# Token loads as two transfers of 48 rows, the sum of f written ahead of its rounded copy, and 24 nudged operations in a spectral transform with a gated FFN on one core

## The chip, the core and the metric

The kernel runs on one core of a Trainium2 chip. The metric is the device time of one execution in microseconds; lower is better. TensorE (PE) does the matrix products, VectorE (DVE), ScalarE (ACT) and GpSimd (POOL) do the element-wise work, and SyncE (SP) issues nearly all DMA transfers.

## The reference

Eight sequences of 3008 tokens with 256 channels go through a spectral layer, and its output through a gated feed-forward layer.

```python
X = np.fft.rfft(x, axis=1)                     # x: (8, 3008, 256), float32
Yr = Xr @ w_r - Xi @ w_i + b_r
Yi = Xr @ w_i + Xi @ w_r + b_i
Yr = sign(Yr) * maximum(abs(Yr) - 0.01, 0)     # and the same for Yi
y = np.fft.irfft(Yr + 1j * Yi, n=3008, axis=1)
g = y @ w_gate                                 # 24064 tokens, 256 -> 1536
silu = g / (1 + exp(-g))
out = (silu * (y @ w_val)) @ w_out             # 1536 -> 256
```

## The kernel before

The program has two stages: the transform (0 to 520 us of the span) and the gated FFN (519 to 2555 us, matmul line L791), which the change leaves as it is.

**Tokens.** The 3008 tokens of a sequence are cut into factors for a Fourier transform done by matrix products. The input is laid out by the host so that one array `xp[b, k]` holds the tokens of sequence b for a pair of chunks k (eight pairs a sequence) as 128 rows of 1024 floats. Rows 0 to 47 and 64 to 111 carry tokens (47 and a zero row each); the other rows are zero. One transfer of 128 rows (512 KB) brings a pair: L332 for sequence 0 (`x_first`), L463 for the others (`x`, written as "scratch<-xp" in the rows). `stage_a` (L470, operation names `first k` for sequence 0 and `tiles k` for the others) multiplies the two 48-row halves by the constant `wa` into two banks; 16 block transposes a sequence on DVE (`turn`, L475) put the result into `d`. The constant `wa` comes with its own small transfer at L309.

**Slots.** There are 8 sequences of 12 pairs of frequencies, 96 slots j in all. Each runs through this chain:

- `second` (PE, L513) writes a bank `ps_b` of 128x512 from `d`;
- `f` (ACT, L576) copies one half of that bank; `f_sum` (DVE, L577) adds the other half to it, the rows "f<-f,ps_b";
- `f_hi` (ACT, L575) rounds the whole bank to the short format; `f_lo` (DVE, L578) forms what the rounding left out, bank less `f_hi`;
- `flat_hi` (ACT, L579) and `flat_lo` (POOL, L580) do the same for the sum f, and `sum` (PE, L520) multiplies them;
- `spread` (DVE, L524) and `mix` (PE, L535) add to the products, `gather` (ACT, L547), `clip` (DVE, L585) and `shrink` (POOL, L586) do the thresholding, `y_hi` and `y_lo` (L587, L594) split again, `back` (PE, L557 and L559) transforms back, `z` and `store` (L598, L599) put the result into `d` in DRAM.

`second j+1` overwrites `ps_b` after `f_lo j` and `f_sum j` have read it.

In the same time PE does `stage_a` for the next sequence, and the last transform step of the one before (`z_in`, transfers at L639 from `d` in two pieces of 48 rows, rows 0 to 47 and 64 to 111, 192 KB each, and the products at L650). DVE and POOL also convert FFN weights (`bits`, L418 to L424).

**Order.** Each operation has a key: its slot times 5.5, moved by a number of its kind from the table `SHIFT`. A planner walks through the operations by key, chooses an engine where there are two, and so fixes each engine's order; nothing is reordered at run time. An operation that is written later and touches the same PSUM bank or buffer waits for the one ahead of it, on whatever engine it runs.

**Start.** All eight `x_first` pairs are loaded first, with `wr`, `wf`, `bias`, `wj` and `raw_i` behind them, and then the pairs of sequence 1 (`x 0` and on). PE does some products on a cleared tile (L719, L721) ahead of `first 0`, and fills its waits with products on such tiles (L740 and L742, "idle").

Of the kernel before, what the change touches and what calls it, by code (L numbers as in the profile page):

```python
# [17 lines left out]
P = 128  # L18
# [27 lines left out]
SHIFT = {"add": -0.5, "lower": 0.5, "third": -0.5, "turn5": 0.12, "turn4": 0.06, "turn0": -0.44, "y_hi": -0.37, "f": -0.5, "out": 0.75, "spread": 0.0, "back": -0.19, "raw": 0.37, "second": 0.06, "y_lo": 0.68, "shrink": 0.44, "z_in": 0.06, "mix": 0.5, "wr": -1.0, "turn1": 0.0, "tiles": 0.56, "turn6": -0.31, "wo": 0.06, "x_sum": -0.5, "sum": -0.5, "flat_lo": -0.12, "xt1": 0.18, "x": 0.12, "store": 0.37, "turn": -0.32, "wm": -0.12, "bits down": -0.5, "upper": 0.25, "wj": -0.12, "kept": -1.0, "negate": 0.25, "turn3": 0.12, "unit": 0.56, "wm_hi": -0.12, "z": 0.5, "bias": -0.44, "wi_lo": -0.06, "turn2": -0.18, "x_hi": -0.5, "clip": -0.5, "xt0": -0.25, "wa": 0.06, "warm": 0.25, "bits up": -1.5}  # L46
# [4 lines left out]
WARM = 1  # L51
# [198 lines left out]
def spectral_ffn(ctx: ExitStack, tc: tile.TileContext, xp, w_r, w_i, cb, wup_raw, wdn_raw, ca, cf, ci, cq, out):  # L250
# [15 lines left out]
    with ExitStack() as tail:  # L266
        last = tail.enter_context(tc.tile_pool(name="last", bufs=2, side="right"))
        with ExitStack() as one:
            finish, stored = transform(one, tc, front, ring, last, ps_, feed, xp, w_r, w_i, cb, wup_raw, wdn_raw, ca, cf, ci, cq, w21, wup_d, wdn_d, xt_d, d2)
# [6 lines left out]
def transform(ctx, tc, front, ring, last, ps_, feed, xp, w_r, w_i, cb, wup_raw, wdn_raw, ca, cf, ci, cq, w21, wup_d, wdn_d, xt_d, d2):  # L276
# [16 lines left out]
    places = [scratch[:, i * T : (i + 2) * T] for i in (3, 5)]  # L293
# [21 lines left out]
    def head(plan):  # L315
# [816 lines left out]
```

## Time and profile before

| | us |
|---|---|
| median of 3 runs (2557.44 to 2557.63) | 2557.52 |
| the profiled execution | 2556.73 |
| its span | 2554.9 |
| PE busy in it | 2544.8 |
| DVE / POOL / ACT busy | 2064.7 / 2082.1 / 1705.0 |

The page of the profile gives busy times and shares for the span. Its 40 slices of 63.9 us show PE at 9 tenths or more in every slice and a granted clock of 9 tenths or more in every slice; the DMA digits are 6 to 8 in the first eight slices and 4 to 5 behind them. The views by window cut the same sums to stretches of our choice. A row of the timeline is one instruction, or some of the same form in a row (x4), with its start, its length, and in brackets how long its engine stood idle ahead of it and what ended that.

### The profile page before, as it was taken

What the parts mean: (1) busy time and instruction counts of PE and PEld (TensorE: products, weight loads), DVE (VectorE), ACT (ScalarE), POOL (GpSimd) and SP (SyncE); (2) the same over time, 40 slices, a digit from 0 to 9 for tenths busy, and PEclk for the clock granted to TensorE, in tenths of its full rate; (3) what the DMA queues carried; (4) which work ended last, traced back from release to release, by engine and by line L of the source; (5) the groups of instructions that cost most, each with busy time, mean ns of one, the idle gap of its engine ahead of it and who ended that gap; (6) DMA issues with size and microseconds to landing.
All of it is one profiled execution on the core that took longest, in us unless ns stands there. A gap on an engine that the chain in (4) does not pass through costs nothing.

```text
span 2554.9 us, 45902 instructions
## 1 busy us (share of the span) xinstructions
PE 2544.8 (100%) x16534; PEld 2136.0 (84%) x16534; DVE 2064.7 (81%) x2998; ACT 1705.0 (67%) x3342; POOL 2082.1 (81%) x1595
## 2 busy tenths in 40 slices
PE   9999999999999999999999999999999999999999
PEld 6888888978888888888888888888888888888899
DVE  7989898677877877887788788878887888788887
ACT  6888888966666665666656666666666566656665
POOL 5777777568888888888888888888888888888886
PEclk9999999999999999999999999999999999999999
DMA  6788888855445444544444444444444444444453
GB/s 236 246 293 277 287 281 273 252 206 183 159 154 177 163 154 153 175 157 151 160 158 150 141 163 163 151 142 163 163 151 143 162 163 146 142 158 158 151 182 123
DMA packets 133924, 460.57 MB, mean 180 GB/s; under 512 B 13632, under 2 KB 58944, under 8 KB 133696
## 3 DMA queue, kind: packets, MB, share of 16 engines
q1 hardware_dynamic: 133552, 457.53, 54.0%
q8 instruction: 131, 2.15, 0.4%
q14 instruction: 97, 0.79, 0.1%
q10 hardware_dynamic: 144, 0.10, 0.0%
HBM read 366.61 MB, written 90.96 MB: 179 GB/s over the span
## 4 chain that ended last, share of the span: by engine, by line
PE 97%; DVE 1%; DMA 1%; ACT 0%; issue 0%; POOL 0%; SPq 0%; DVEq 0%
PE bank L791 79%; PE mixb L535 5%; PE ps_b L513 3%; PE ps_s L520 3%; PE ps_z L559 3%; PE ps_x L650 2%; PE ps_a L470 2%; PE bank L1037 0%; DMA x_first<-xp 0%; DMA scratch<-xp 0%; PE ps_z L557 0%; DVE y_lo L594 0%; ACT t L547 0%; DVE f_lo L578 0%; POOL t L586 0%
## 5 line engine op out<-in xcount | busy, mean ns | idle before, releaser
L791 PE MATMUL bank<-x_near,wup 128*128 128x512 f32 (+1 forms) x4032 | 1035.8, 386 | 0.4 <-DVE bank L964 0.2
L811 POOL TENSOR_TENSOR h_parts<-more,h_parts 128x512 fp32r<-128x512 f32 (+1 forms) x572 | 847.2, 1495 | 101.8 <-ACT h_parts L807 100.7
L791 PEld LDWEIGHTS bank<-x_near,wup 128*128 128x128 f32 x4032 | 751.0, 188 | 152.7 <-DVE bank L964 3.9
L791 PE MATMUL bank<-h_parts,wdn 128*128 128x512 f32 (+1 forms) x3024 | 835.3, 385 | 0.0
L811 POOL TENSOR_TENSOR h_parts<-hidden,h_parts 128x512 fp32r<-128x512 f32 (+1 forms) x431 | 563.7, 1319 | 213.7 <-ACT h_parts L807 176.9
L791 PEld LDWEIGHTS bank<-h_parts,wdn 128*128 128x128 f32 x3024 | 564.9, 188 | 108.5 <-POOL h_parts L811 0.3
L807 ACT CAST h_parts<-hidden 128x512 fp32r<-128x512 f32 (+1 forms) x433 | 265.5, 613 | 451.0 <-DVE hidden L937 449.7
L791 PE MATMUL bank<-x_parts,wup 128*128 128x512 f32 (+1 forms) x2016 | 525.7, 384 | 0.0
L937 DVE TENSOR_TENSOR hidden<-hidden,bank 128x512 f32<-128x512 f32 (+1 forms) x576 | 375.8, 674 | 78.1 <-PE bank L791 69.6
L791 PEld LDWEIGHTS bank<-x_parts,wup 128*128 128x128 f32 x2016 | 375.4, 188 | 71.7 <-DVE bank L964 1.7
L832 DVE TENSOR_TENSOR sums<-sums,bank 128x512 f32<-128x512 f32 (+1 forms) x357 | 240.2, 673 | 234.3 <-PE bank L791 234.3
L807 ACT CAST h_parts<-more 128x512 fp32r<-128x512 f32 (+1 forms) x572 | 349.3, 611 | 39.3 <-DVE more L802 28.4
L935 ACT ACTIVATE hidden<-bank 128x512 f32<-128x512 f32 (+1 forms) x432 | 252.6, 585 | 114.6 <-PE bank L791 113.9
L802 DVE TENSOR_TENSOR more<-hidden 128x512 f32<-128x512 f32 (+1 forms) x286 | 291.9, 1059 | 0.0
L802 DVE TENSOR_TENSOR more<-hidden,more 128x512 f32<-128x512 f32 (+1 forms) x286 | 257.7, 901 | 0.0
L942 ACT COPY bank<-bank 128x512 f32<-128x512 f32 (+1 forms) x288 | 161.6, 561 | 109.3 <-DVE hidden L937 103.9
L964 DVE TENSOR_TENSOR bank<-hidden,bank 128x512 f32<-128x512 f32 (+1 forms) x288 | 196.9, 684 | 36.3 <-PE bank L791 23.5
L586 POOL TENSOR_TENSOR t<-t,y 128x512 f32<-128x512 f32 x94 | 129.3, 1376 | 70.1 <-DVE y L585 63.1
L950 ACT COPY hidden<-bank 128x512 f32<-128x512 f32 (+1 forms) x288 | 167.6, 582 | 2.2
L547 ACT COPY t<-mixb 64x256 f32<-64x256 f32 x384 | 140.9, 367 | 22.0 <-PE mixb L535 17.1
L243 POOL TENSOR_TENSOR x_near<-xf,x_near 128x512 fp32r<-128x512 f32 (+1 forms) x112 | 142.3, 1286 | 5.2 <-PE bank L791 4.8
L986 DVE TENSOR_TENSOR hidden<-hidden,bank 128x512 f32<-128x512 f32 (+1 forms) x144 | 97.4, 676 | 42.7 <-PE bank L791 42.4
(111 smaller groups left out, 3104.1 us busy)
## 6 DMA issues: line engine op xcount, KB each, us to landing
wup<-wup_d SPq DMA_DIRECT2D x288, 896.0 KB, 4.7
scratch<-xp SPq DMA_DIRECT2D x59, 512.0 KB, 4.9
out<-o SPq DMA_DIRECT2D x88, 256.0 KB, 6.1
d<-z SPq DMA_DIRECT2D x84, 256.0 KB, 3.9
z_in<-d SPq DMA_DIRECT2D x112, 192.0 KB, 5.1
xt_d<-xt SPq DMA_DIRECT2D x56, 376.0 KB, 4.7
xf<-xt_d SPq DMA_DIRECT2D x15, 1024.0 KB, 7.8
wup_d<-wup SPq DMA_DIRECT2D x12, 896.0 KB, 5.8
```

The source lines that it names most:

```text
L243: low = lambda: eng.tensor_tensor(part[:, 1, :h], src, f32(part[:, 0, :h]), op=ALU.subtract)
L547: nc.scalar.copy(t()[64 * half : 64 * half + 64, k * C : (k + 1) * C], mixb[64 * k : 64 * k + 64, half * C : (half + 1) * C])
L791: nc.tensor.matmul(o, lhsT=weights[w], rhs=parts[x], start=start and i == 0, stop=stop and i == 2, skip_group_check=True)
L802: v.tensor_tensor(at(o, h), at(a, h), at(b, h), op=ALU.subtract)
L807: act.copy(pair[i][:, 0, :h], at(i, h))
L811: eng.tensor_tensor(pair[i][:, 1, :h], at(i, h), f32(pair[i][:, 0, :h]), op=ALU.subtract)
L832: v.tensor_tensor(o, o, spare[:, :h], op=ALU.add)
L935: act.activation(at(i, h), src, AF.Silu)
L937: v.tensor_tensor(at(i, h), at(i, h), src, op=ALU.mult)
L942: act.copy(b3[:, :h], b1[:, :h])
L950: act.copy(m5, b2[:, :h])
L964: v.tensor_tensor(b2[:, :h], m5, b3[:, :h], op=ALU.add)
```

## The change

The change has four parts.

1. **Transfers of 48 rows.** Every pair of tokens is loaded as two transfers, rows 0 to 47 and rows 64 to 111, 192 KB each, in place of one of 128 rows. The zero rows are not moved any longer. `wa` travels with the first pair (48 rows of 1088 floats), and POOL copies it from there to its own tile; its transfer is gone.
2. **f_sum ahead of f_hi.** After planning, the order in which the operations are written is gone through: where it can be done without passing another operation of ACT, or of DVE, `f_hi j` is put behind `f_sum j`.
3. **Tables.** `SHIFT`, `BIAS` and the keys of `wr` and `wj` have new values, and 24 single operations get a further shift of 0.25 or 0.5 slot (`NUDGE`).
4. **Start.** The clearing of the tile for PE's first products goes from POOL to DVE, with other numbers of these products; the differences and sums of the weights (`wm`, `wm_lo`) may go to DVE or POOL; the second of two banks is cleared by an operation of its own.

```diff
-BIAS = {'y_lo POOL': 0.2, 'z DVE': 1.7, 'flat_lo DVE': 1.2, 'shrink DVE': 1.5}
+BIAS = {"y_lo POOL": 0.1, "z DVE": 0.7, "flat_lo DVE": 1.5, "shrink DVE": 1.6}
+NUDGE = {"shrink 33": -0.5, "flat_lo 17": -0.25, "tiles 41": 0.25, "turn 0 3": 0.5,
...
-        key += SHIFT.get(name.split()[0], 0) * SLOT
+        key += (SHIFT.get(name.split()[0], 0) + NUDGE.get(name, 0)) * SLOT
...
+    HALVES = slice(0, 48), slice(64, 112)
...
-            nc.sync.dma_start(box[k], xp[0, k, :, : 2 * T])
+            wide = 2 * T if k else 2 * T + 64
+            if not k:
+                box[k] = scratch[:, 5 * T : 5 * T + wide]
+            for rows in HALVES:
+                nc.sync.dma_start(box[k][rows], xp[0, k, rows, :wide])
...
-        plan.add("wa", "SP", 0.45, -39.5, [], load_wa, 2.0)
+        plan.add("wa", "POOL", 0.2, -39.5, ["x_first 0"], lambda: [g.tensor_copy(wa[rows], box[0][rows, 2 * T :]) for rows in HALVES])
...
-        plan.add("wm 1", "POOL", 1.23, 0.5 * SLOT, ["wj"], combine(1, ALU.subtract))
+        plan.add("wm 1", either, None, 0.5 * SLOT, ["wj"], combine(1, ALU.subtract), wide=True)
...
     def fetch(t, b, k):
-        nc.sync.dma_start(t, xp[b, k, :, : 2 * T])
+        for rows in HALVES:
+            nc.sync.dma_start(t[rows], xp[b, k, rows, : 2 * T])
...
     order = plan.order()
+    for j in range(B * NP):
+        names = [name for name, _ in order]
+        i, k = names.index(f"f_hi {j}"), names.index(f"f_sum {j}")
+        between = {engine for _, engine in order[i + 1 : k]}
+        if i < k and "ACT" not in between:
+            order.insert(k, order.pop(i))
+        elif names.index(f"f {j}") < i < k and "DVE" not in between:
+            order.insert(i, order.pop(k))
```

**The start on PE.** This is PE's order from the later pairs of sequence 0 to `second 1`; L470 (L477 after) is `first` and `tiles`, L513 (L520) is `second`, L740 and L742 (L760 and L762) are the filling products. Before:

```order
L470 MATMUL ps_a<-x_first,wa 64x512 x20
L470 MATMUL ps_a<-scratch,wa 64x512 x4
L740 MATMUL mixb_130<-warm,wa 64x128 x2
L740 MATMUL mixb_131<-warm,wa 64x128 x2
L740 MATMUL mixb_130<-warm,wa 64x128 x2
L740 MATMUL mixb_131<-warm,wa 64x128 x2
L513 MATMUL ps_b<-wf,d_0_115 128x128 x2
L742 MATMUL mixb_130<-warm 128x128 x2
L513 MATMUL ps_b<-wf,d_0_115 128x128 x2
L742 MATMUL ps_x_249<-warm 128x128 x5
L470 MATMUL ps_a<-scratch,wa 64x512 x4
L513 MATMUL ps_b<-wf,d_0_115 128x128 x4
```

and after:

```order
L477 MATMUL ps_a<-x_first,wa 64x512 x12
L728 MATMUL mixb_131<-warm 128x512
L520 MATMUL ps_b<-wf,d_0_115 128x128 x2
L762 MATMUL mixb_130<-warm 128x128
L477 MATMUL ps_a<-scratch,wa 64x512 x4
L760 MATMUL mixb_130<-warm,wa 64x128 x4
L477 MATMUL ps_a<-scratch,wa 64x512 x4
L520 MATMUL ps_b<-wf,d_0_115 128x128 x2
L762 MATMUL ps_x_287<-warm 128x128 x8
L520 MATMUL ps_b<-wf,d_0_115 128x128 x4
```

The first four matmuls of "scratch" are the last pair of sequence 0, the next four are `tiles 0`, the first of sequence 1. Before, both halves of `second 0` stood ahead of `tiles 0`; after, its first half stands ahead of the last pair of sequence 0, and its second half behind `tiles 0`.

**The start on SP.** This is the order of the first transfers. Before:

```order
L332 DMA scratch<-xp 128x1024
L309 DMA wa<-ca 128x64
L332 DMA scratch<-xp 128x1024
L332 DMA x_first<-xp 128x1024 x5
L332 DMA scratch<-xp 128x1024
L350 DMA wr<-w_r 128x2x256
L313 DMA wf<-cf 128x768
L350 DMA bias<-bias 128x512
L350 DMA wj<-w_i 128x2x256
L350 DMA raw_i<-ci 128x256
L463 DMA scratch<-xp 128x1024 x2
```

and after:

```order
L335 DMA scratch<-xp 48x1088 x2
L335 DMA scratch<-xp 48x1024 x2
L335 DMA x_first<-xp 48x1024 x10
L335 DMA scratch<-xp 48x1024 x2
L312 DMA wf<-cf 128x768
L353 DMA wr<-w_r 128x2x256
L353 DMA bias<-bias 128x512
L353 DMA wj<-w_i 128x2x256
L353 DMA raw_i<-ci 128x256
L470 DMA scratch<-xp 48x1024 x4
```

The sequence is the same but for `wr`, which stands behind `wf`; sixteen transfers of 48 rows stand where eight of 128 rows and `wa` stood.

**One slot on ACT and DVE.** These are ACT's rows of slot 33 (about 181 us), with the waits written into the instructions. Before:

```order
L576 COPY f<-ps_b 128x256 [waits PE_49]
L575 CAST f_hi<-ps_b 128x4x2x64
L579 CAST f_hi<-f 128x256 [waits DVE_49]
L587 CAST y_hi<-t 128x512 [waits Pool_49]
L547 COPY t<-mixb_131 64x256 [waits PE_49]
```

and after:

```order
L583 COPY f<-ps_b 128x256 [waits PE_49]
L582 CAST f_hi<-ps_b 128x4x2x64 [waits DVE_49]
L586 CAST f_hi<-f 128x256
L594 CAST y_hi<-t 128x512 [waits Pool_49]
L554 COPY t<-mixb_131 64x256 [waits PE_49]
```

ACT's order is the same, but the rounded copy now waits for DVE, whose sum the third instruction then needn't wait for. In 87 of the 96 slots the copy waits so after the change, in 13 before. DVE's rows of the same slot, from the transpose ahead of them, were

```order
L475 STREAM_TRANSPOSE d_1_116<-ps_a 128x16x16x2 [waits PE_49]
L577 TENSOR_TENSOR f<-f,ps_b 128x256 [waits PE_49,Activation_49]
L578 TENSOR_TENSOR f_lo<-ps_b,f_hi 128x4x2x64
L524 TENSOR_TENSOR mixb_130<-ps_s,bias 128x512 [waits PE_49]
L475 STREAM_TRANSPOSE d_1_116<-ps_a 128x16x16x2
```

and are

```order
L482 STREAM_TRANSPOSE d_1_116<-ps_a 128x16x16x2 [waits PE_49]
L584 TENSOR_TENSOR f<-f,ps_b 128x256 [waits Activation_49]
L585 TENSOR_TENSOR f_lo<-ps_b,f_hi 128x4x2x64 [waits Activation_49]
L531 TENSOR_TENSOR mixb_130<-ps_s,bias 128x512 [waits PE_49]
L482 STREAM_TRANSPOSE d_1_116<-ps_a 128x16x16x2
```

Nothing moved on DVE, but `f_lo` now has a wait of its own on ACT: the copy that it needs comes behind the sum that DVE has just done. Such a wait stands in 87 slots; in 72 of these the sum and `f_lo` are neighbours on DVE, in 15 another operation stands between them.

From 20 to 400 us PE's order is otherwise the same as before; behind 400 us a few products move by one to three places. The FFN's order is unchanged.

## Rows read from the trace of the kernel before

**Rows 1.** The page: the span, and the busy times of the engines.

```profile
span 2554.9 us, 45902 instructions
...
PE 2544.8 (100%) x16534; PEld 2136.0 (84%) x16534; DVE 2064.7 (81%) x2998; ACT 1705.0 (67%) x3342; POOL 2082.1 (81%) x1595
```

**Rows 2.** Windows: length, PE, PEld, DVE, ACT, POOL busy (x), clock, DMA share, GB/s.

```profile
0.00:20.00 20.00, 16.25 (x116) 7.13 (x116) 10.66 (x18) 4.65 (x10) 4.17 (x8) 1.00 0.91 338
...
100.00:400.00 300.00, 299.91 (x4391) 261.08 (x4390) 268.42 (x445) 253.83 (x598) 236.92 (x214) 1.00 0.88 283
```

**Rows 3.** PE's timeline in the start: start us, length, instruction, idle before it.

```profile
14.78 1.09 PE L470 MATMUL ps_a<-scratch,wa 48*64 48x512 f32 x8 [0.25 <-DMA scratch<-xp]
...
17.45 0.64 PE L513 MATMUL ps_b<-wf,d 128*128 128x128 f32 x4
17.93 1.28 PE L742 MATMUL ps_x<-warm 128*128 128x128 f32 x10
19.45 1.09 PE L470 MATMUL ps_a<-scratch,wa 48*64 48x512 f32 x8 [0.24 <-DMA scratch<-xp]
20.47 1.21 PE L513 MATMUL ps_b<-wf,d 128*128 128x128 f32 x8
21.43 0.36 PE L520 MATMUL ps_s<-wm_hi,f_hi 128*128 128x256 f32 x1
...
23.78 1.18 PE L513 MATMUL ps_b<-wf,d 128*128 128x128 f32 x8 [0.37 <-DVE f_lo L578]
```

**Rows 4.** Windows of two stretches, with the columns of rows 2.

```profile
100.40:103.20 2.80, 2.80 (x23) 2.59 (x21) 2.78 (x6) 2.41 (x6) 1.97 (x2) 1.00 0.84 198
8.00:14.00 6.00, 5.18 (x44) 1.16 (x40) 6.00 (x11) 0.00 (x0) 0.00 (x0) 1.00 1.03 414
```

**Rows 5.** SP's timeline: the z_in transfers issued ahead of the first of these stretches.

```profile
96.14 2.19 SPq L639 DMA_DIRECT2D z_in<-d  x4
```

**Rows 6.** The timeline of one slot, f_hi ahead of f_sum (slot 33).

```profile
180.78 0.38 ACT L576 COPY f<-ps_b 128x256 f32<-128x256 f32 x1
...
181.05 0.59 ACT L575 CAST f_hi<-ps_b 128x512 fp32r<-128x512 f32 x1
...
181.68 0.42 DVE L577 TENSOR_TENSOR f<-f,ps_b 128x256 f32<-128x256 f32 x1 [1.57 <-ACT f_hi L575]
...
182.01 0.68 DVE L578 TENSOR_TENSOR f_lo<-ps_b,f_hi 128x512 fp32r<-128x512 f32 x1
...
182.84 0.36 PE L513 MATMUL ps_b<-wf,d 128*128 128x128 f32 x1
```

**Rows 7.** The timeline of a slot with f_sum ahead of f_hi (slot 81).

```profile
435.01 0.37 ACT L576 COPY f<-ps_b 128x256 f32<-128x256 f32 x1 [0.27 <-PE ps_b L513]
...
435.42 0.42 DVE L577 TENSOR_TENSOR f<-f,ps_b 128x256 f32<-128x256 f32 x1 [0.36 <-ACT f L576]
...
435.87 0.59 ACT L575 CAST f_hi<-ps_b 128x512 fp32r<-128x512 f32 x1
...
436.49 0.69 DVE L578 TENSOR_TENSOR f_lo<-ps_b,f_hi 128x512 fp32r<-128x512 f32 x1
```

**Rows 8.** ACT's waits of the whole span: total us, times, longest.

```profile
ACT f_hi L575 <- DVE f L577: 1.1, 5, 0.3
```

**Rows 9.** DVE's groups by form in 100 to 400 us: busy, mean ns | idle before.

```profile
L578 DVE TENSOR_TENSOR f_lo<-ps_b,f_hi 128x512 fp32r<-128x512 f32 x57 | 38.8, 681 | 0.5 <-ACT f_hi L575 0.4
...
L577 DVE TENSOR_TENSOR f<-f,ps_b 128x256 f32<-128x256 f32 x57 | 23.8, 417 | 24.4 <-ACT f_hi L575 20.1 <-issue 1.9 <-POOL scratch L430 1.0
```

**Rows 10.** The timeline of a slot in which DVE comes late (slot 46).

```profile
248.02 1.24 DVE L422 SCALAR_TENSOR_TENSOR scratch<-scratch 128x512 f32<-128x512 int32 x1
...
249.68 0.68 DVE L578 TENSOR_TENSOR f_lo<-ps_b,f_hi 128x512 fp32r<-128x512 f32 x1
...
250.51 0.47 PE L513 MATMUL ps_b<-wf,d 128*128 128x128 f32 x2
```

**Rows 11.** PE's timeline: the last such slot (73), its second after f_lo.

```profile
393.62 0.35 PE L513 MATMUL ps_b<-wf,d 128*128 128x128 f32 x1
```

More of the change, by code (lines that the diff above doesn't have):

```diff
@@ L45 @@
 FEED = 84
-SHIFT = {"add": -0.5, "lower": 0.5, "third": -0.5, "turn5": 0.12, "turn4": 0.06, "turn0": -0.44, "y_hi": -0.37, "f": -0.5, "out": 0.75, "spread": 0.0, "back": -0.19, "raw": 0.37, "second": 0.06, "y_lo": 0.68, "shrink": 0.44, "z_in": 0.06, "mix": 0.5, "wr": -1.0, "turn1": 0.0, "tiles": 0.56, "turn6": -0.31, "wo": 0.06, "x_sum": -0.5, "sum": -0.5, "flat_lo": -0.12, "xt1": 0.18, "x": 0.12, "store": 0.37, "turn": -0.32, "wm": -0.12, "bits down": -0.5, "upper": 0.25, "wj": -0.12, "kept": -1.0, "negate": 0.25, "turn3": 0.12, "unit": 0.56, "wm_hi": -0.12, "z": 0.5, "bias": -0.44, "wi_lo": -0.06, "turn2": -0.18, "x_hi": -0.5, "clip": -0.5, "xt0": -0.25, "wa": 0.06, "warm": 0.25, "bits up": -1.5}
+SHIFT = {"add": -0.5, "lower": -0.51, "third": -0.5, "turn5": -0.88, "turn4": -0.89, "turn0": -1.26, "y_hi": -0.01, "f": -0.12, "out": 0.3, "spread": 0.0, "back": -0.68, "raw": 1.24, "second": -0.06, "y_lo": 0.74, "shrink": 0.87, "z_in": 0.07, "mix": 0.5, "wr": -0.73, "turn1": -0.49, "tiles": 0.74, "turn6": -1.67, "wo": -1.61, "x_sum": 0.2, "sum": -1.49, "flat_lo": 0.19, "xt1": 0.55, "x": 0.3, "store": 0.8, "turn": -0.26, "wm": -1.05, "bits down": -0.5, "upper": 1.03, "wj": 0.88, "kept": -1.19, "negate": 2.3, "turn3": -0.02, "unit": 2.32, "wm_hi": 0.32, "z": 0.45, "bias": 0.16, "wi_lo": 2.13, "turn2": 1.03, "x_hi": 0.25, "clip": -0.5, "xt0": -1.08, "wa": 1.42, "warm": -0.56, "bits up": -1.5, "xf": -0.88, "early": -1.06, "gather": -0.01, "first": 1.37, "clear": -1.25, "sums": 0.56, "x_first": -0.39, "wm_lo": -1.78, "bits": -0.2, "x_lo": -1.49, "wi_hi": -1.61, "raw_i": 0.77, "wf": -0.44, "f_hi": 0.18, "flat_hi": 0.19, "f_lo": 0.06}
 REACH = 160
 LOOSE = 95
-BIAS = {'y_lo POOL': 0.2, 'z DVE': 1.7, 'flat_lo DVE': 1.2, 'shrink DVE': 1.5}
+BIAS = {"y_lo POOL": 0.1, "z DVE": 0.7, "flat_lo DVE": 1.5, "shrink DVE": 1.6}
+NUDGE = {"shrink 33": -0.5, "flat_lo 17": -0.25, "tiles 41": 0.25, "turn 0 3": 0.5, "f_sum 67": -0.25, "xt0 8": 0.5, "spread 84": -0.25, "bits up 10": 0.25, "gather 42": 0.25, "f_hi 86": 0.25, "out 8": -0.25, "turn4 up 7": 0.25, "z_in 21": -0.25, "turn2 up 4": 0.5, "flat_lo 33": 0.25, "turn4 up 9": -0.25, "z_in 49": -0.25, "back 52": 0.25, "mix 40": -0.5, "xt0 23": -0.25, "mix 73": -0.25, "turn 6 14": -0.25, "kept up 6": 0.5, "sum 91": -0.25}
 SLOT = 5.5
-WARM = 1
 FULL = 40.0
@@ L268, in spectral_ffn @@
         with ExitStack() as one:
[L269 removed]
+            finish, stored = transform(one, tc, front, ring, last, ps_, feed, xp, w_r, w_i, cb, wup_raw, wdn_raw, cf, ci, cq, w21, wup_d, wdn_d, xt_d, d2)
         finish()
@@ L292, in transform @@
     stored = []
-    places = [scratch[:, i * T : (i + 2) * T] for i in (3, 5)]
+    places = [scratch[:, i * T : (i + 2) * T] for i in (5, 3)]
     def take():
@@ L715, in transform, with clear @@
     warm = k1p.tile([P, T], F32, name="warm")
-    nc.gpsimd.memset(warm, 0.0)
-    nc.scalar.activation(warm[:, 0:1], warm[:, 0:1], AF.Silu)
-    for _ in range(WARM):
-        nc.tensor.matmul(mixed[0][:, :C], lhsT=warm[:, :P], rhs=warm[:, C:], start=True, stop=True)
-    for bank in mixed:
-        nc.tensor.matmul(bank, lhsT=warm[:, :P], rhs=warm, start=True, stop=True)
+    table = k1p.tile([P, 1], F32, name="table")
+    v.memset(warm, 0.0)
+    nc.gpsimd.memset(table, 0.0)
+    nc.scalar.activation(table, table, AF.Silu)
+    def clear(bank, cols=T):
+        nc.tensor.matmul(mixed[bank][:, :cols], lhsT=warm[:, :P], rhs=warm[:, :cols], start=True, stop=True)
+    for _ in range(2):
+        clear(0, P)
+    clear(0)
+    plan.add("clear", "PE", 0.87, -1.0, ["turn 0 10", "turn 0 11"], lambda: clear(1))
     plan.add("warm", "ACT", 0.2, -50, [], lambda: None)
@@ L737, in idle @@
             for half in range(2):
-                rows = slice(64 * half, 64 * half + 48)
+                rows = slice(0, 48)
                 for g in range(2):
-                    nc.tensor.matmul(mixed[half][64 * g : 64 * g + 64, :P], lhsT=wa[rows], rhs=warm[rows, :P], start=False, stop=True, skip_group_check=True)
+                    nc.tensor.matmul(bank[64 * g : 64 * g + 64, half * P : half * P + P], lhsT=wa[rows], rhs=warm[rows, :P], start=False, stop=True, skip_group_check=True)
         else:
```

42 lines of the change are left out of this document (21 added, 21 removed).

## The prediction

> **What bounds the kernel now.** I read the page's busy times first. PE is busy for 2544.8 of 2554.9 us and no other engine, weight loads apart, passes 81% [rows 1]; so a change pays only if it takes products from PE or fills the 10.1 us in which PE stands idle, and it costs where it makes PE wait anew. The windows by stage come next. In 100 to 400 us PE misses 0.09 of 300 us, at a clock of 1.00 (the 2.4 GHz level); beside it DVE is busy for 268.42, ACT for 253.83, and the DMA share is 0.88 [rows 2]. That stretch has nothing to give, and two neighbours that are nearly full. The first 20 us hold 3.75 us of PE's idle time and a part of its busy time is filling [rows 2, 3]. The third view is PE's timeline in that start, to see which wait ends last: the last pair of sequence 0 reaches PE at 14.78, `tiles 0` begins when its transfer lands at 19.45, both straight behind a DMA wait; `second 1` follows at 20.47 and the first `sum` at 21.43 [rows 3]. Transfers set the start. Last come the timelines of single slots, to see how closely `second j+1` follows `f_lo j`: in slot 33 `f_lo` ends at 182.69 and `second 34` begins at 182.84, 0.15 later, without any idle time of PE [rows 6].
>
> **The 48-row transfers in the start.** Eight pairs of 128 rows are 4.19 MB; as halves they are 2 x 48 x 4352 + 14 x 48 x 4096 bytes = 3.17 MB. At an equal rate this would be a gain. The rate of 128-row pairs is 414 GB/s (8 to 14 us, share 1.03) [rows 4]. The nearest rows for a queue that holds nothing but 48-row halves are those of `z_in`: four of them issued from 96.14 on [rows 5], and in 100.4 to 103.2 us the core moves 198 GB/s at a share of 0.84 [rows 4], so its engines are engaged and slow. The other end is the same engines in mixed traffic: 283 GB/s at a share of 0.88 over 300 us [rows 2], or 322 GB/s of busy time, with such halves in it. The start holds sixteen halves in a row, so I take 198. Then 3.17 MB need 16.0 us. Before, the 4.19 MB were there at 14.6, and at 414 GB/s they take 10.1: 4.4 us go into the first issue and the ramp. A slower stream loses less in a ramp, so I put 3.0 there (1.9 to 4.4, an estimate): the last pair is there at 19.0 instead of 14.6. Behind it stand 1.28 MB of weights in 128 rows (3.1 us at 414 GB/s) and `x 0`, 393 KB at 198 GB/s (2.0 us): 24.1, and `tiles 0` starts at 24.3 instead of 19.45. By the new order the second half of `second 0` stands behind it: 24.3 + 1.09 = 25.4 instead of 17.45. Of this the filling gives something back, since it is eight single products of 0.128 us (1.0) [rows 3]: `second 1` comes at 25.4 + 0.5 + 1.0 = 26.9 instead of 20.47, +6.4. The first `sum` needs the split of f 0, which takes some 3.0 us from that half on: 28.4 instead of 21.43, **+7.0**. From there PE has no gap in which the delay could be made good. Bounds: with the share at 1, 198 / 0.84 = 236 GB/s, and the short ramp it is 4 us less, +3; the long ramp gives +8.4; with full-speed transfers DVE's last transposes set the start and the term is about 0 (rival two). `wm 1` ahead of DVE's last two transposes needs `wj`, which lands ahead of `x 0` on the same queue, so it sets nothing while the transfers are slow. POOL's copies of `wa` (two of 48 x 64) lie behind the first pair's landing and ahead of the second's, and `first 0` reads the landed copy: nothing; without that cover they would cost under 1 us.
>
> The row says 198 GB/s for halves, the mixed stretch 322, so a rule is of use beside it. The Trainium skill, page "SBUF — State Buffer", section "Door 1: The DMA port swizzle (why `[64,N]` ≈ `[32,N]`)", has it that a transfer to the first 64 partitions alone reaches half of the ports, 196 GB/s measured there, and "Can I just issue two DMAs to hit both halves?" adds only some 6% for a pair of halves. By it the 3.17 MB would need 15.2 to 16.2 us, an estimate from that page, and the term would be +6 to +7; the z_in rows agree, the mixed stretch does not show it.
>
> **The 48-row transfers later.** A pair as two halves takes 393 KB / 198 = 1.98 us instead of 512 KB / 410 = 1.28, +0.7. Some 38 pairs lie in 100 to 400 us: 27 us of 300 if none overlaps, and the share of 0.88 [rows 2] would rise to about 0.97. Pairs are fetched ahead into several buffers and PE loses 0.09 us there in all, so most of this is cover used up, not time. Where it runs out are the seven changes of sequence, at which `z_in` halves and pairs compete: up to 0.8 each. From 0 to +6; I take **+1**, near the low end, as the row shows no transfer wait. SP's doubled issues cost nothing on the path: 0.55 us each (2.19 us for four) [rows 5], for some 100 more issues in 500 us.
>
> **f_sum ahead of f_hi.** Both read the bank `ps_b`, and the one written later waits for the other: before, f_sum starts 0.04 after f_hi ends (181.64 and 181.68) although f was ready at 181.16 [rows 6]; with the order turned ACT's f_hi waits for f_sum, five times, 0.3 us at most [rows 8]. `f_lo` needs f_hi, so a step of DVE now stands ahead of the ACT step on which f_lo hangs. Counted from f's start, old order: f_hi 0.27 to 0.86, f_sum 0.90 to 1.32, f_lo ends at 1.91 [rows 6]. New order, as slot 81 already has it: f_sum 0.41 to 0.83, f_hi 0.86 to 1.45, f_lo ends at 2.17 [rows 7]. So f_lo comes 0.25 later if DVE is free at once. Where DVE comes late, the old order had f_hi done by then and the new one has not: in slot 46 the weight conversion holds DVE to 249.26, f_sum runs 0.42 from about 249.34 to 249.76, f_hi would run from 249.79 to 250.38 and f_lo start at 250.41 instead of 249.68 [rows 10], +0.7. The sum path (flat_hi, flat_lo) comes no later, since flat_hi stands behind both f_sum and f_hi in either order.
>
> Who waits for f_lo: `second j+1`. I looked through the slots whose order changes for those where it starts under 0.2 us behind f_lo, as in slot 33: 17, from slot 1 (`second 2` at 23.78, waiting 0.37 for f_lo) [rows 3] to slot 73 (393.62) [rows 11]. In 10 DVE is early (10 x 0.25 = 2.5), in 2 between (2 x 0.37 = 0.7), in 5 late (5 x 0.7 = 3.5): 6.7 us, if lateness doesn't pass from slot to slot. The floor is 17 x 0.25 = 4.3. But DVE now stands idle between f_sum and f_lo for 0.03 + 0.59 + 0.03 = 0.65 where the two are neighbours, which is 43 of the 57 slots in 100 to 400 us: 28 us, while the 24.4 us in which it stood idle ahead of f_sum [rows 9] are what is given up for it. 268.4 + 28 = 296 of 300: DVE is all but full, so it is mostly late, and 17 x 0.7 = 11.9 is the other end. I take **+10**, nearer to the late end. ACT loses up to 0.58 a slot behind its waiting f_hi (y_hi and gather are queued there), 33 us in 57 slots on top of 253.83: it just fits into 300 and comes second to DVE.
>
> **Tables and nudges.** PE's order from 20 to 400 us is unchanged but for these; behind 400 a few products move by one to three places, where no PE wait stands now: 0, bounds -0.5 and +0.5. The FFN is untouched: 0.
>
> **Sum.** 7.0 + 1 + 10 = +18.0 on the profiled execution's 2556.73: 2574.7. The runs' median is 0.8 above that execution, so 2575.5.
>
> **Rivals.**
> *One: halves move at full speed, f chain as above.* In the start the queue always holds both halves of several pairs, and if the engines drift apart the two halves are served together, as the 322 GB/s of mixed traffic allow. Then the start costs 0, and the rest +10 (+8 to +13): 2567, slower by more than 0.2%.
> *Two, ending on the other side: halves move at full speed and therefore the whole change is not slower.* At 414 GB/s `x 0` lands near 16.5, DVE's last transposes and `wm 1` end at about 17.9, the second half of `second 0` follows, and the filling that is shorter by 0.3 gives `second 1` near 19.5: the start gains 0.4 to 0.9. With transfers no tighter than now and DVE catching up between slots the f chain stays at its floor of 4.3: 2557.5 + 4.3 - 0.6 = 2561, within 0.2% (5.1 us). It decides when a pair of halves takes under about 1.1 us in the start.
> *Three: halves slow, but the f chain absorbed.* DVE regains its 0.65 us by running other work earlier, and only the floor or less is paid: 2557.5 + 7 + 1 + 1 = 2566.
> *Four: the order does not do what it says*, f_sum finding the bank free beside f_hi; then f_lo starts as before or 0.1 earlier, and the time is that of case three. The waits against it are in rows 6 and 8, so it is counted there.
>
> **How the numbers follow.** Forecast (halves slow, f chain paid, 2568 to 2584): 0.66. Rival one (2565 to 2571): 0.10. Rival two (2559 to 2562.6): 0.13. Three and four (2563 to 2568): 0.08. Faster by some gain that no row shows: 0.03. A measurement of this kernel tells 0.2%, 5.1 us, from no change. So faster 0.03, same 0.13, slower 0.84. The range goes from 2561, which takes in case two's centre, to 2584, where all terms stand at their upper ends (8.4 + 6 + 12 = 26.4 on 2557.5); it leaves out about 0.15.
>
> **What would show it.** Right: `tiles 0` of sequence 1 at 24 to 25 us on PE with a DMA wait ahead of it, under 230 GB/s in 4 to 18 us; f_hi 0.03 behind f_sum in most slots; PE waiting for f_lo at `second` for some 10 us in all; DVE idle ahead of f_lo, not ahead of f_sum. Wrong: the pairs of the start arriving under 1.2 us apart, or PE still missing under 1 us in 100 to 400 us. The sum fails too if TensorE, left waiting in the start, is granted its lower level of 1.2 GHz there, which no row of before shows, or if pairs come late at every change of sequence (+6).

## The result, and the profile after

The changed kernel takes 2584.76 us (median of 4 runs, 2583.94 to 2587.97) against 2557.48 (4 runs, 2557.41 to 2557.63) for the kernel before: 1.0109 times as long, 95% interval 1.0093 to 1.0125, or +27.3 us. The prediction had said slower, 2575.5 with a range up to 2584: the sign was right, the size a third too small, and the range was missed by 0.8 us. The profiled execution took 2584.16.

The page and the windows by stage of the kernel after, which answer to [rows 1, 2]; the columns are the same:

```profile
span 2582.4 us, 46122 instructions
...
PE 2558.0 (99%) x16556; PEld 2141.8 (83%) x16556; DVE 2067.9 (80%) x3006; ACT 1701.4 (66%) x3341; POOL 2070.2 (80%) x1591
...
0.00:20.00 20.00, 17.30 (x110) 7.60 (x110) 10.86 (x17) 3.09 (x6) 2.04 (x8) 1.00 0.94 250
...
100.00:400.00 300.00, 290.07 (x4116) 250.01 (x4114) 255.77 (x426) 242.00 (x574) 222.92 (x203) 1.00 0.85 256
```

PE now misses 9.93 us of the 300, where it missed 0.09. DVE and ACT are not busier in that stretch, they are less busy; they wait. The waits of the three engines in 100 to 400 us of the kernel after (total us, times, longest):

```profile
PE ps_b L520 <- DVE f_lo L585: 5.0, 8, 1.2
PE ps_s L527 <- ACT z L605: 3.0, 7, 0.7
PE ps_z L566 <- DVE mixb L531: 0.7, 3, 0.4
...
ACT f_hi L582 <- DVE f L584: 36.1, 45, 1.7
...
DVE f_lo L585 <- ACT f_hi L582: 28.6, 44, 0.7
```

The row of DVE's f_lo is the 0.65 us a slot that the prediction had put between f_sum and f_lo: 28.6 us in 44 slots, forecast 28 in 43. The row of ACT is new in size; it had 1.1 us in five slots over the whole span [rows 8]. ACT now stands still for 36.1 us because f_hi waits for a sum on DVE, up to 1.7 at a time. And PE waits not for f_lo alone, but also for `z`, which ACT writes, and for the bank that `spread` writes on DVE ("mixb").

To see where the time was lost I set the start of `f` in each slot of one kernel against that of the same slot before. The kernel after is 5.5 us late in slot 0, 6.2 in slot 4, 22.6 in slot 75, 27.8 in slot 95, and 27.5 at the end of the span. So the start costs 6, the middle of the transform 16.5, its end 5, and the FFN nothing. The profiled execution of before is 0.8 us under its median; kernels below whose start is that of before are 0.6 to 1.1 late in slot 0 by this measure, so about 1 us of the 5.5 is not the change.

PE's timeline in the start, the answer to [rows 3]:

```profile
20.56 1.90 PE L477 MATMUL ps_a<-scratch,wa 48*64 48x512 f32 x8 [1.14 <-DMA scratch<-xp]
22.39 1.18 PE L520 MATMUL ps_b<-wf,d 128*128 128x128 f32 x4
23.36 3.16 PE L762 MATMUL ps_x<-warm 128*128 128x128 f32 x16
26.36 1.11 PE L520 MATMUL ps_b<-wf,d 128*128 128x128 f32 x8
27.22 0.36 PE L527 MATMUL ps_s<-wm_hi,f_hi 128*128 128x256 f32 x1
...
29.73 1.21 PE L520 MATMUL ps_b<-wf,d 128*128 128x128 f32 x8 [0.54 <-DVE f_lo L585]
```

`tiles 0` starts at 20.56, only 1.1 later than before and far from the 24.3 that I had forecast. But it then takes 1.90 instead of 1.09, the second half of `second 0` 1.18 instead of 0.64, and the filling 3.16. The row of `tiles 0`, asked for in two narrow windows, comes apart into the products of the two halves of 48 rows:

```profile
20.56 1.08 PE L477 MATMUL ps_a<-scratch,wa 48*64 48x512 f32 x4 [1.14 <-DMA scratch<-xp]
...
21.39 1.07 PE L477 MATMUL ps_a<-scratch,wa 48*64 48x512 f32 x4
```

Before, the four products of the one half start within 0.02 us of those of the other and run beside them. Now the second half lands at 21.25, 0.73 behind the first, and its products start 0.83 later; the granted clock in 20 to 22 us is still 1.00. For the rest, windows of the same kernel tell why, and at what rate the halves came:

```profile
8.00:14.00 6.00, 5.40 (x50) 2.51 (x48) 4.26 (x7) 0.00 (x0) 0.00 (x0) 1.00 1.03 263
20.00:22.00 2.00, 1.44 (x8) 0.42 (x8) 2.00 (x3) 0.77 (x2) 1.68 (x2) 1.00 1.06 284
22.00:24.00 2.00, 2.00 (x10) 1.61 (x8) 1.45 (x2) 0.37 (x1) 0.28 (x1) 0.62 0.98 370
24.00:26.00 2.00, 2.00 (x11) 2.00 (x11) 1.34 (x3) 1.53 (x4) 0.05 (x1) 0.53 1.06 281
```

The halves move at 263 GB/s at a share of 1.03, between the 198 that I had taken and the 414 of 128-row pairs [rows 4]; and from 22 to 26 us the granted clock is 0.62 and 0.53, that is mostly its lower level of 1.2 GHz, behind 1.14 us in which PE waited for `x 0`. `second 0` and the filling lie in there.

### The profile page after: what moved, and what is told of

The parts are those of the page before. It is cut to its first block, busy times and chain, and to the rows that moved or that the text cites. A ratio compares the mean times of both kernels' runs of the same rounds, so it can differ in the third digit from the quotient of the medians.

```text
span 2582.4 us, 46122 instructions
## 1 busy us (share of the span) xinstructions
PE 2558.0 (99%) x16556; PEld 2141.8 (83%) x16556; DVE 2067.9 (80%) x3006; ACT 1701.4 (66%) x3341; POOL 2070.2 (80%) x1591
## 4 chain that ended last, share of the span: by engine, by line
PE 88%; DVE 5%; ACT 3%; issue 2%; POOL 1%; DMA 1%; SPq 0%; DVEq 0%; POOLq 0%; ACTq 0%
PE bank L811 78%; PE mixb L542 2%; PE ps_b L520 2%; PE ps_z L566 1%; PE ps_s L527 1%; PE ps_x L657 1%; PE ps_a L477 1%; DVE d L482 1%; ACT f_hi L582 1%; DVE f_lo L585 1%; ACT t L554 1%; DVE f L584 1%; DVE y_lo L601 1%; DVE mixb L531 1%; DVE y L592 1%
## 5 line engine op out<-in xcount | busy, mean ns | idle before, releaser
L831 POOL TENSOR_TENSOR h_parts<-more,h_parts 128x512 fp32r<-128x512 f32 (+1 forms) x572 | 847.3, 1495 | 101.2 <-ACT h_parts L827 100.4
```

Of the source, the lines that this page charges most:

```text
L831: eng.tensor_tensor(pair[i][:, 1, :h], at(i, h), f32(pair[i][:, 0, :h]), op=ALU.subtract)
```

## The experiments

Times are medians; each is compared with the kernel before in the same set of runs (2556.97 to 2557.46). Delays by slot are worked out as above.

### Which part costs

**The pass taken out.** Removed from the changed kernel:

```diff
-    for j in range(B * NP):
-        names = [name for name, _ in order]
...
-            order.insert(i, order.pop(k))
```

> The changed kernel without the pass that puts f_sum ahead of f_hi; all else stays. Theory F (the 17.5 us lost between slots 4 and 74 come from that order): about 2567 us (2565 to 2570), and PE misses under 1 us in 100 to 400 us again. Theory D (they come from the 48-row transfers): 2582 or more. The start costs its 6 us in both.

2563.65 us (ratio 1.0027, 1.0017 to 1.0037), so the pass costs 21.1 us in the changed kernel. In 100 to 400 us PE is left with two of its waits:

```profile
PE ps_b L520 <- DVE f_lo L585: 0.5, 1, 0.5
PE ps_s L527 <- ACT z L605: 0.4, 1, 0.4
```

**The pass alone**, the same lines added to the kernel before.

> The kernel before with that pass alone. Theory F: 2557.5 + 15 to 18 = 2572 to 2576, with waits of PE for f_lo at second and for z at sum. Theory D: 2557 to 2560. My prediction had +10 for this (4.3 to 11.9).

2580.65 us (1.0093, 1.0078 to 1.0108): +23.5. The delay goes from 0.9 us in slot 0 to 17.9 in slot 75 and 25.9 in slot 95. Of this 3.8 lie between slots 92 and 95, where PE stood idle for 1.50 and then had a clock of 0.68 in 524 to 528 us; the profiled execution was the slowest of the four. Theory F's cause holds, its range of 2572 to 2576 was too low, and the term is more than twice my +10 and twice the upper end that I had given it.

**128-row transfers in the changed kernel**, with its order kept:

```diff
-            for rows in HALVES:
-                nc.sync.dma_start(box[k][rows], xp[0, k, rows, :wide])
+            nc.sync.dma_start(box[k], xp[0, k, :, :wide])
...
-        for rows in HALVES:
-            nc.sync.dma_start(t[rows], xp[b, k, rows, : 2 * T])
+        nc.sync.dma_start(t, xp[b, k, :, : 2 * T])
```

> The changed kernel with the tokens in transfers of 128 rows, in the same order. Theory D: 2570 or less. Theory F, with a start that is lost to order and clock: 2582 to 2584, the first pair of sequence 1 lands about 1 us earlier, and the granted clock still falls. If the start is lost to the transfers: 2579.

2579.58 us (1.0088, 1.0073 to 1.0103): the halves cost 5.2 in the changed kernel. This was the time named for a start that is lost to the transfers, but not all of it lies there: in the profiled executions this kernel is 2.2 us ahead of the changed one in slot 0, 2.8 in slot 72 and 4.5 in slot 95. The clock does not fall at 22 us here, against what I had expected; it is down to 0.57 in 8 to 12 us instead, behind 1.61 us in which PE waited for an `x_first` pair.

**Halves alone**, the opposite edit to the kernel before, for all pairs.

> The kernel before with the tokens in two transfers of 48 rows, order unchanged. Theory D: 2568 or more. Theory F: 2558.5 to 2560.5, as tiles 0 would start near 20.6 instead of 19.45 and PE waits for no transfer later. My prediction's start (198 GB/s) would give 2563 to 2565.

2560.73 us (1.0017, 1.0007 to 1.0026), with single executions from 2558.3 to 2565.9. The profiled one took 2564.14. Its rate is near the one that I had forecast, its clock is not:

```profile
5.00:15.00 10.00, 9.96 (x45) 2.63 (x45) 5.74 (x9) 0.00 (x0) 0.00 (x0) 0.92 1.04 193
15.00:20.00 5.00, 5.00 (x24) 1.61 (x22) 3.45 (x5) 0.11 (x1) 0.00 (x0) 0.50 1.03 220
20.00:26.00 6.00, 6.00 (x40) 5.17 (x32) 1.58 (x3) 2.16 (x5) 3.76 (x3) 0.50 1.08 267
```

193 GB/s, a half every 1.02 us, and a clock of 0.50 over more than ten microseconds; `tiles 0` starts at 27.11, behind filling and not behind a transfer. So the same transfers run at 193 GB/s in one program and at 263 in another. The delay is 7.7 us in slot 1 and 7.6 in slot 92: in between, 91 slots with some 50 pairs in halves cost nothing.

**What is left**: both edits, no pass and 128 rows, on the changed kernel.

> The changed kernel with 128-row transfers and without the pass: what is left are the tables, the nudges and the start's new order. If the parts add up: 2584.8 - 5.2 - 21.1 = 2558.5 (2557 to 2560).

2559.04 us (1.0008, 0.9999 to 1.0017), +2.1, not clear of no change. The parts add up: 21.1 + 5.2 + 2.1 = 28.4 against 27.3. The 2.1 lie in the start's new order (slot 0 is 2.9 late in the profiled execution); from slot 1 (2.6 late) to slot 72 (2.4) nothing is added, and behind it the tables and nudges move the delay between 1.1 and 3.9, to end at 2.4 in slot 95 and 1.7 at the end of the span.

### In which slots the pass costs

The prediction had priced 17 slots in which `second j+1` stands under 0.2 us behind f_lo. The pass in these alone:

```diff
+    for j in range(B * NP):
+        if j not in (1, 2, 6, 23, 25, 33, 36, 38, 43, 46, 49, 57, 60, 62, 67, 70, 73):
+            continue
```

> The kernel before with the pass in the 17 slots alone in which my prediction saw second close behind f_lo. Theory P (these slots are what costs, the price was only too low): most of the 23 us, 2572 or more. Theory A (the pass costs through ACT's queue, in all slots): own price of f_lo at second, 17 slots x 0.25 to 0.7, 2562 to 2566.

2563.29 us (1.0022, 1.0012 to 1.0032): +5.8. The price worked out from the rows was 6.7. Slot 33 [rows 6] and slot 46 [rows 10] in this kernel, on the timeline:

```profile
183.72 0.59 ACT L575 CAST f_hi<-ps_b 128x512 fp32r<-128x512 f32 x1 [0.49 <-DVE f L577]
...
184.34 0.69 DVE L578 TENSOR_TENSOR f_lo<-ps_b,f_hi 128x512 fp32r<-128x512 f32 x1 [0.65 <-ACT f_hi L575]
...
185.09 0.39 PE L513 MATMUL ps_b<-wf,d 128*128 128x128 f32 x1
...
252.82 0.59 ACT L575 CAST f_hi<-ps_b 128x512 fp32r<-128x512 f32 x1 [0.81 <-DVE f L577]
...
253.44 0.69 DVE L578 TENSOR_TENSOR f_lo<-ps_b,f_hi 128x512 fp32r<-128x512 f32 x1 [0.66 <-ACT f_hi L575]
...
254.19 0.39 PE L513 MATMUL ps_b<-wf,d 128*128 128x128 f32 x1 [0.44 <-DVE f_lo L578]
```

Counted from f's start, the 17 starts of `second` slip by 0.15 to 0.21 where DVE is early and by 0.43 to 0.58 where it is late, where I had 0.25 and 0.7, since of the 0.15 that lay between f_lo and `second` 0.1 is used up first. Together the slips make 4.7. This half of the step was right.

**The pass in all slots but these 17.**

> The kernel before with the pass in all slots but those 17. Theory P: 2557 to 2562. Theory A: 2557 + 12 to 17 = 2569 to 2574, with waits of PE for z at sum and at back.

2573.14 us (1.006, 1.0042 to 1.0078): +15.7 where the prediction had nothing at all. These slots I split by DVE in the trace of before: 35 in which it is still busy with earlier work 0.1 to 1.8 us after f is ready, and 20 in which it is free (two are in neither). First the late ones:

> The kernel before with the pass in 35 of the other slots: those in which DVE is still busy with earlier work when f is ready (by 0.1 to 1.8 us in the trace of before). Theory L (f_hi, once it waits for a late DVE, stalls ACT with all that is queued behind it): 12 to 15 us of the 15.7, 2570 to 2573. Theory E (each turned slot costs the same): 35 / 55 of it, +10, 2567.

2569.02 us (1.0047, 1.0032 to 1.0062): +12.1. Then the early ones:

> The kernel before with the pass in the other 20 slots, in which DVE is free when f is ready. Theory L: 2557 to 2560. Theory E: +6, 2563.

2563.50 us (1.0025, 1.0014 to 1.0036): +6.5, three times what theory L allowed, and what theory E had said. In medians a turned slot costs 12.05 / 35 = 0.34 us late, 6.5 / 20 = 0.33 early, 5.8 / 17 = 0.34 tight. By slot it isn't so even: the transform alone, from slot 0 to the first product of the FFN, loses 12.2 in the late slots, 5.9 in the tight ones, 3.0 in the early ones; with the early ones another 2.7 us of that profiled execution lie in the FFN. There the same products, with no wait of PE over 0.2 us, fall behind evenly, 0.6 us in the first 550 us and 2.7 in 1930, so it is no wait that the pass made; why they do I did not find. This also is why late and early slots make 18.6 one by one and 15.7 together.

### What the late slots pay for

One place of the kernel with the pass in late slots, ACT, DVE and PE on the timeline:

```profile
232.71 0.37 ACT L576 COPY f<-ps_b 128x256 f32<-128x256 f32 x1
...
235.24 0.58 ACT L575 CAST f_hi<-ps_b 128x512 fp32r<-128x512 f32 x1 [1.66 <-DVE f L577]
235.72 0.62 ACT L587 CAST y_hi<-t 128x512 fp32r<-128x512 f32 x1
236.24 1.50 ACT L547 COPY t<-mixb 64x256 f32<-64x256 f32 x4
...
238.93 0.60 ACT L598 COPY z<-ps_z 128x512 f32<-128x512 f32 x1
...
233.08 1.79 DVE L594 TENSOR_TENSOR y_lo<-t,y_hi 128x512 fp32r<-128x512 f32 x1
234.79 0.41 DVE L577 TENSOR_TENSOR f<-f,ps_b 128x256 f32<-128x256 f32 x1
235.85 0.69 DVE L578 TENSOR_TENSOR f_lo<-ps_b,f_hi 128x512 fp32r<-128x512 f32 x1 [0.65 <-ACT f_hi L575]
236.46 0.69 DVE L524 TENSOR_TENSOR mixb<-ps_s,bias 128x512 f32<-128x512 f32 x1
...
237.21 0.50 PE L559 MATMUL ps_z<-y_hi,wi_hi 128*128 128x512 f32 x1 [0.20 <-DVE mixb L524]
...
239.59 0.39 PE L520 MATMUL ps_s<-wm_hi,f_hi 128*128 128x256 f32 x1 [0.48 <-ACT z L598]
```

and the same slot before:

```profile
227.18 0.60 ACT L575 CAST f_hi<-ps_b 128x512 fp32r<-128x512 f32 x1
...
231.65 0.59 ACT L598 COPY z<-ps_z 128x512 f32<-128x512 f32 x1
...
228.51 0.41 DVE L577 TENSOR_TENSOR f<-f,ps_b 128x256 f32<-128x256 f32 x1
...
232.31 0.37 PE L520 MATMUL ps_s<-wm_hi,f_hi 128*128 128x256 f32 x1
```

f is ready at 233.08, DVE is in `y_lo` until 234.87, its sum ends at 235.20, and only then may ACT round the bank. Before, ACT began to round it 1.33 us ahead of the sum. Behind the waiting f_hi stand `y_hi`, four `gather`, `flat_hi`, two copies of `xt` and `z` on ACT, and the next `sum` on PE needs the bank that this `z` empties: PE waits 0.48 us for it. f_lo has no part in this wait. It has one in another: DVE stands idle for 0.65 ahead of f_lo, `spread` comes behind f_lo on DVE, and `back` on PE waits 0.20 for spread. So the lateness goes on through two queues.

To tell ACT's stall from f_lo and from a full DVE, three kernels keep the old order and add needless work. First a copy on ACT behind f_hi in 73 of the 74 slots that the pass turns:

```diff
+    pad = k1p.tile([P, T], F32, name="pad")
...
+            order.insert(names.index(f"f_hi {j}") + 1, ("pad", "ACT"))
...
+        if name == "pad":
+            return nc.scalar.copy(pad, pad)
```

> The kernel before, old order, with a needless ACT copy of 128x512 (0.59 us) behind f_hi in the 73 slots that the pass would turn. f_lo is not later than before; ACT loses what it loses in the changed kernel, and flat_hi, y_hi, gather and z come later. Theory A: +10 us or more (2568 to 2575). Theory P: 0 to +2.

2561.80 us (1.0017, 1.0007 to 1.0026): +4.3, between the two theories. An even 0.59 us a slot is mostly swallowed by ACT's slack. Then a subtraction on DVE ahead of f_lo in the same slots:

> The kernel before, old order, with a needless DVE subtraction of 128x512 (0.68 us) ahead of f_lo in the same 73 slots. f_lo comes 0.65 later and DVE is as full as in the changed kernel, while ACT waits for nothing new. Theory P: +10 to +12 at least (2568 to 2572) as in the prediction. Theory A: +6 to +8, as at second in the kernel with the pass.

2607.99 us (1.0198, 1.0182 to 1.0214): +50.5. Two wait rows and the window of 100 to 400 us:

```profile
PE ps_b L513 <- DVE f_lo L578: 15.0, 13, 2.8
PE ps_z L559 <- DVE mixb L524: 4.6, 9, 1.1
...
100.00:400.00 300.00, 275.58 (x3891) 237.95 (x3891) 281.83 (x442) 231.98 (x544) 218.70 (x194) 0.99 0.80 255
```

This outruns every theory, and the fault is the kernel's: it keeps DVE's waiting ahead of f_sum (20 us, [rows 9]) and adds its own time on top, where the pass gives up the first for the second. It shows how little room DVE has, and that a later DVE makes `back` wait for `spread`, not what the pass takes of it. The last one puts on ACT, in the 35 late slots alone, about as many copies as f_hi would have waited there (1 to 4, 70 in all).

> The kernel before, old order, with ACT kept busy behind f_hi in the 35 late slots for about as long as it would wait for f_sum there (1 to 4 needless copies of 0.59 us, 70 in all). f_lo is not later and DVE has nothing to add. If ACT's stall is what the late slots cost: 2565 to 2570, with PE waiting for z at sum as in the kernel with the pass in these slots. If f_lo or DVE is: 2557 to 2561.

2577.01 us (1.0079, 1.0064 to 1.0094): +20.0, though f_lo is not later and DVE has nothing added. Its waits of PE in 40 to 520 us:

```profile
PE ps_s L520 <- ACT z L598: 12.5, 12, 2.6
PE ps_z L559 <- DVE mixb L524: 1.0, 3, 0.4
```

Nearly as many copies as in the even case (70 against 73) cost nearly five times as much when they come in lumps. The lumps were heavier than the real waits: 70 copies of 0.59 are 41 us, where ACT's f_hi waits 31.0 us for DVE in the kernel with the pass in the late slots; and behind a wait of 2.56 PE's clock fell to 0.72 in 108 to 112 us, which it does nowhere in that kernel. So the run shows that an ACT that stalls in lumps makes `sum` wait for z, at the place where the kernel with the pass shows it. It does not show that this is all that the late slots lost, for that kernel waits at `back` as well, in the same 40 to 520 us:

```profile
PE ps_s L520 <- ACT z L598: 3.8, 10, 0.7
PE ps_z L559 <- DVE mixb L524: 2.8, 9, 0.7
PE ps_b L513 <- DVE f_lo L578: 1.2, 1, 1.2
```

Before, these three are 0.3, 0.4 and 0.5. How much each path costs can be read from the traces, since PE's products of the transform keep their order in these kernels. The start of each product is set against the start of the same product in the kernel without the pass (or without the copies), from slot 4 on, and each new delay is booked on what that product waited for:

| PE waits at | the pass, in the changed kernel | the pass in the late slots | ACT copies in lumps |
|---|---|---|---|
| `sum`, for z on ACT | 6.4 | 5.8 | 15.4 |
| `second`, for f_lo | 5.6 | 0.7 | 0 |
| `back`, for spread on DVE | 3.0 | 3.1 | 0.7 |
| the last transform step, for `xt` on ACT | 0.9 | 0.8 | 0.7 |
| `sum`, for POOL | 2.0 | 0.4 | 0.2 |
| others, and gaps too short to be booked | 4.1 | 1.3 | 2.4 |
| in all (us, rounded) | 22.0 | 12.2 | 19.4 |

The path through ACT to z is the largest of three, and not the only one. The lumps on ACT make the first path show by itself; the path through DVE to spread rests on these delays and on the row of `back` above.

### The opposite order

Before, 13 slots already had f_sum first. The opposite pass puts f_hi ahead in 12 of these as well.

> The kernel before with the opposite pass: f_hi ahead of f_sum also in the slots in which before has f_sum first (13 of them). If the order itself costs even there, 2555 to 2557; if the planner chose these slots where DVE is early enough or late work hides it, 2557 to 2558.

2562.11 us (1.002, 1.0011 to 1.003): +5.1, outside of both cases. Its waits of PE in 40 to 520 us:

```profile
PE ps_z L559 <- DVE mixb L524: 4.6, 9, 0.8
```

In these slots f_hi is the late one: DVE waits up to 2.31 us for it at f_sum (slot 21), `spread` stands behind that on DVE, and `back` on PE waits for spread. So neither order is good as such.

### The start

**Halves in sequence 0 alone.**

> The kernel before with two transfers of 48 rows for the pairs of sequence 0 alone. If all that the halves cost is in the start: 2559 to 2562, as with all pairs in halves, with executions between 2558 and 2566. If the later pairs cost too: 2558.

2561.16 us (1.0017, 1.0007 to 1.0026), +4.2, in two heaps: five executions at 2559.0 to 2559.6, five at 2562.8 to 2563.8. The profiled one is of the lower; 222 GB/s in 5 to 15 us, no fall of the clock, 2.4 to 2.8 us late from slot 0 to the end.

**Halves in the later sequences alone.**

> The kernel before with two transfers of 48 rows for the pairs of sequences 1 to 7 alone. If all that the halves cost is in the start: 2557 to 2558. By my prediction's term: 2558 (2557 to 2563).

2560.53 us (1.0013, 1.0003 to 1.0022), +3.5, from 2558.2 to 2563.4: against my expectation these cost as much as the first eight, and each set costs as much as both together. But all of it lies in the start: the profiled execution is 1.6 us late in slot 0, 7.2 in slot 4 and 7.2 in slot 92. On PE:

```profile
21.78 2.68 PE L471 MATMUL ps_a<-scratch,wa 48*64 48x512 f32 x8 [1.41 <-DMA scratch<-xp]
24.39 2.07 PE L514 MATMUL ps_b<-wf,d 128*128 128x128 f32 x8
```

`x 0`, the first pair of sequence 1, is one of the halves that stand on the path in the start. PE waits 1.41 us for it, and soon works at half speed (granted clock 0.50 in 26 to 32 us; `second 1` takes 2.07 instead of 1.21).

**The weights' sums back on POOL**, in the changed kernel:

```diff
-        either = {"POOL": 1.23, "DVE": 0.61}
+        either = {"POOL": 1.23}
```

> The changed kernel with the sums of the weights on POOL again. DVE doesn't wait for wj ahead of the last two transposes, and both halves of second 0 are followed by half the filling. If that wait and the filling behind it set the start beside slow halves: 2 to 3 us less than the changed kernel, 2582. If the halves alone set it: 2584 to 2585.

2588.66 us (1.0123, 1.0108 to 1.0138): 3.9 more than the changed kernel, not 2 to 3 less. Slot 0 is 8.2 late instead of 5.5. The planner also orders what follows otherwise, so that the pass turns 62 slots and not 74, and up to 23 us PE's rows are longer (the first half of `second 0` takes 1.06 instead of 0.63). So the 3.9 are not the cost of this edit alone, and whether DVE's wait for `wj` has a part in the start stays open.

## Why the prediction was right or wrong

**The wait that the f order makes was right, the path from it to PE was not.** The step that failed is the one from the two neighbours to PE: that ACT "just fits into 300 and comes second to DVE", and that a later DVE costs at `second` alone. I had worked out that ACT would lose up to 0.58 us a slot, 33 in 57 slots (measured: 36.1 in 45), and then let it go, because the sum still fitted. The sum over 300 us does not decide. ACT loses by lumps of up to 1.7 us, where DVE is late, and an engine that works in order hands such a lump to everything that stands behind: `z`, and by it `sum` (6.4 us of the pass's 22.0 in the changed kernel). I had named y_hi and gather as queued there and not followed the queue as far as z. DVE's idle 0.65 ahead of f_lo goes on in the same way to `spread`, and by it to `back` (3.0), where I had nothing either. So the term that I put at +10, in 17 slots, is 5.8 in these 17 and 15.7 in the others: 21 to 23.

**The 17 tight slots were right**, 5.8 against 6.7. What I added to reach 10 (all 17 at the late price, because DVE is nearly full) stands for nothing that the runs show: they kept an early and a late price in the kernel that turns them alone, and with the pass in all slots PE's delay for f_lo at `second` is still 5.6.

**The wait itself was right.** f_hi waits for f_sum on the bank that both read. The Trainium skill, page "PSUM — Partial Sum Buffer", section "PSUM bank collisions raise a hardware error ⚠️", has it that the compiler's scheduler adds a dependency between any two instructions on different engines that touch the same 32 partitions of a bank, reads and writes alike; the trace agrees, with 45 such waits of f_hi in 300 us.

**The start: the size nearly right, by luck.** Forecast +7.0, and 5.5 to 6 by slots. The 198 GB/s that I took was 263 here; `tiles 0` came at 20.6, not 24.3. What filled the gap I had at nothing or only among the ways to fail: the two halves of `tiles 0` run one behind the other (0.8), and in 22 to 26 us the clock is lower, behind a wait of 1.14 us, with a `second 0` that takes nearly twice as long and 3.16 us of filling. Of the filling I had counted eight products, 1.0 us, from the order, where the trace counts two for each instruction of the order: 16.

The row of 198 GB/s I had also misread. Its window, 100.4 to 103.2 us, does not hold halves alone: SP issued a store of 256 KB of z at 100.34, and 256 of the window's 369 packets are between 512 bytes and 2 KB, where a row of a half has 4 KB. That the kernel with halves alone then came near it, with 193, is luck as well.

By the Trainium skill, page "SBUF — State Buffer", sections "Door 1: The DMA port swizzle (why `[64,N]` ≈ `[32,N]`)" and "Can I just issue two DMAs to hit both halves?", a transfer to partitions 0 to 63 moves 196 GB/s, and two, one on each half, only some 6% more together: 196 to 208, as an estimate. The kernel with halves alone agrees with 193; 222 and 263 in the others do not.

**The later halves**: +1 (0 to 6) forecast. In the kernels with halves alone nothing is measured: from slot 4 to slot 92 they stay level to 0.5 us. In the changed kernel they took 2.3 behind slot 0 (4.5 less 2.2 in the profiled executions). Product by product against the same kernel with 128 rows, 0.6 of it is one wait of PE for a `z_in` transfer, at 179.93, and 1.45 one gap within a `sum`, at 495.37; the profile puts this on a POOL operation that had ended 0.9 earlier, so its cause is open. **Tables and nudges**: 0 forecast, 2.1 left over, with an interval that takes in nothing; by slots it lies in the start's new order, which I had priced with the transfers.

**The sum** was 7 + 1 + 10; the runs say some 5.5 (the start, by slot 0), some 2 (later halves) and 21. The f term alone was 11 us too low, more than the whole miss of 9.3. Rival two, with halves at full speed and the pass at 4.3, was further off than the forecast on both counts.

## What to carry to other kernels

Where two engines read one bank, the one whose instruction is written second inherits the lateness of the other's queue and hands it to all that it has queued; put first, slot by slot, the reader whose engine is free first, and turn no order by a rule for all slots: turning 74 slots one way cost 23 us, turning 12 the other way 5, and the planner's mix of before is the best order measured here. When a change adds a wait to an engine with slack, do not compare its busy time and the wait with the span; follow the queue behind the waiting instruction to the first one that the bounding engine needs, and do so on each engine that waits anew, here ACT and DVE. Fewer bytes on fewer partitions were no gain: a quarter less data arrived later, and the bounding engine paid once more in clock for the wait.

## What the runs showed of the hardware

The 48-row transfers of the start moved at 193 and 222 GB/s in the two programs with the start of the kernel before, and at 259 to 263 in the three with the start of the changed one, all at a DMA share of 1.03 to 1.04, against 400 for 128 rows in 5 to 15 us of the kernel before; and executions of one such program fell into heaps 4 us apart, where the kernel before stays within 2556.4 to 2558.5 in 19 runs beside it. What sets the rate, no run here tells.

The products of the two 48-row halves of a pair run beside each other when both are there: eight take 1.09 us in the kernel before. With the halves landing 0.73 us apart they took 1.90, at a granted clock of 1.00.

The granted clock fell to its lower level in the start for 3 to 14 us in kernels in which PE had waited for about a microsecond or more there (1.14, 1.41 and 1.61 us in the three named above, 1.00 in the changed kernel without the pass), and in the kernel with all halves, whose products were strung out between landing halves (0.50 from some 13 to 27 us). Neither is enough by itself: the kernel with halves in sequence 0 alone had its products strung out as well and kept 1.00, and so did the one with copies in lumps behind a wait of 1.14 us, at 125.47. In the kernel before, PE's waits in the start are 0.37 us at most but for the first, and the clock stays at 1.00.
